# Retention attention and a top-1 expert layer on one core: x's rows a block later, the last three blocks routed as one group, weight pieces in other blocks

## The chip, the cores and the metric

The kernel runs on one core of a Trainium2 chip. The metric is device time in microseconds (us) for one execution, of which the median of several runs is given. The core has five engines that each work through their own instructions in order: TensorE (PE, with its weight loads PEld), VectorE (DVE), ScalarE (ACT), GpSimd (POOL) and SyncE (SP, which here only issues DMA transfers). They wait for each other by semaphores. An engine's order is fixed when the kernel is built, so an instruction that waits holds up all that stand behind it on its engine.

## The reference, cut to what matters

```python
# q, k, v: (4, 8, 768, 64); gamma = 1 - 2**(-5 - head)
for t in range(S):
    state = gamma * state + k[t] v[t]^T        # per batch and head, 64 x 64
    y[t] = scale * q[t] @ state
x = y as (3072 tokens, 512)                     # 8 heads x 64
idx = argmax(x/|x| @ (emb/|emb|).T / tau)       # 1 of 8 experts for each token
gate = softmax(...)[idx]
out = gate * (relu(x @ w1[idx]) @ w2[idx])      # w1 512x1024, w2 1024x512
```

Every token goes through one expert only. So tokens have to be counted and sorted by expert, and the rows of x gathered in that order, before an expert's matmuls can start.

## The kernel before, in words

*Attention (lines 860 to 935).* The 3072 tokens are 24 blocks of 128 (NB = 24, six to a batch). The loop over n runs blocks 0 to 22, and block 23 follows behind it by hand, with the first matmuls of the experts already woven in. A block on PE is: `scores` (L349), transposes of the next q and k (L322, L337), `state` (L371), `logits` of the block before (L444), `inter` (L390) and `intra` (L399). DVE multiplies the scores by the causal mask in two halves (`masks`, pm, L356), which `intra` reads. ACT copies the result to xT (`take`). DVE turns xT into rows (`rows`, x, L414), which SP stores to DRAM as xd, two blocks at a time; ACT squares them and DVE sums them (`squares`, `sums`, L431) for the norms. POOL scales q and v (L309, L315). In the kernel before, `rows(n - 1)` and `sums(n - 2)` are called at the end of block n.

*Routing.* For groups of blocks, `to_rows` (PE, L540) and `choose` (DVE, L556 to L570, eight instructions) find the expert of each token, `count` (PE, L578 to L582) counts, `ranks` and `place` (DVE, L589 to L476) give each token its place in its expert's list, `marks_of` prepares the last factor (L489 on POOL, L492 on DVE), and `fill` (PE, L512) with `add_to_table` (DVE, L522 to L525) adds the group to the table of token numbers. Tables are filled at n = 12, n = 18 and n = 21 (18 blocks: the early rows) and once more behind block 23. `pad()` (L603) then makes up the first expert's count to 288 early rows. The blocks behind the early ones are routed in three groups: A = 18 to 20, BB = 21 and 22, CC = 23.

*The hand-over.* `xge` holds the first 288 rows of expert 0, gathered from xd as soon as the table of the early rows stands (L531). `early_rows` transposes them (L669) and splits each number into a high and a low part (xh, xl), since every product of the experts is made of three matmuls: whi with xh, whi with xl, wlo with xh. `products()` is the list of expert 0's single matmuls on the early rows: 96 of the first layer (L219) and 24 for each column block dt of the second (L954). `run(m)` issues m of them, and the tuple R says how many stand at each of the places between the routing steps. `weave` issues several lists of routing instructions in turn.

*Late rows and expert 1.* Behind the last table the 128 late rows of expert 0 are gathered (L1019), transposed (L1040), and run through the first layer (L1055); ACT and DVE make hh and hl of them (L1070), and `late_rows` (L1190, 24 matmuls) is their second layer. `gather(1)` (L236) fetches the rows of expert 1 from xd, they are stored to xs and read back as xg (L246, L252), DVE transposes them (xt, L1114), ACT and DVE split them (xh, xl, L1116, L1118), and expert 1's first layer follows. The gates are gathered as gt (L1090) and multiply the result (L1195). Expert e+2 is gathered while e runs.

*Weights.* A weight piece is 128 x 1024 numbers, eight to an expert. `load_piece` asks SP for the next (512 KB), `split_piece(engine, parts)` lets ACT cast it to whi (L194) and the named engine subtract the two for wlo (L195). Up to the seam POOL does the subtracting in two halves of 128 x 512.

*What sets the order.* In the attention loop and in the seam the instructions of each engine stand as the code issues them, and lists of jobs (`mids`, `lates`, `ends`) put routing steps at fixed places of fixed blocks. In the part behind it a scheduler moves instructions of one engine past each other where their data allow it, so that the diff alone does not tell what stands first.

## Time and profile before

| | |
|---|---|
| three runs | 445.16, 446.98 and 448.91 us; median 446.98 |
| profiled execution | 448.59 us, of which the profile spans 446.8 |
| PE busy | 411.7 us (92% of the span), 3535 matmuls |
| DVE, ACT, POOL busy | 257.3, 177.8, 215.6 us (58%, 40%, 48%) |
| mean clock granted to PE | 0.976 of full speed |
| DMA | 88.16 MB, mean 197 GB/s |

The profile is of one execution. Times in it are us from the span's start. An engine's row in a timeline gives its start, its length, the line of the kernel, the operation with the tiles that it writes and reads, how many alike are merged (x4), and in brackets for how long the engine had been idle and which instruction or transfer ended this. Matmuls overlap, so the length of one is more than its distance to the next. Attention runs to about 127 us, the seam from there to about 156, and the experts from there to the end.

### The profile page before, as it was taken

The numbers are of one execution on the slowest core, as the hardware profiler recorded it, in microseconds if no ns is written. First come the engines' busy times: TensorE is split into PE (matmuls) and PEld (weight loads), VectorE is DVE, ScalarE is ACT, GpSimd is POOL, SyncE is SP. The second block draws the span as 40 slices with busy tenths as digits, with TensorE's granted clock in tenths as the row PEclk, the third lists the DMA queues.
The fourth block names the chain that finished last, engine by engine and source line by source line (L and its number), as shares of the span: only waits on it lengthen the run. The fifth ranks groups of instructions, "written<-read, shape, count | busy, mean of one in ns | idle before, by whom it ended". The sixth has DMA issues, their size and how long they took to land.

```text
span 446.8 us, 9424 instructions
## 1 busy us (share of the span) xinstructions
PE 411.7 (92%) x3535; PEld 366.4 (82%) x3535; DVE 257.3 (58%) x546; ACT 177.8 (40%) x324; POOL 215.6 (48%) x206
## 2 busy tenths in 40 slices
PE   7999999999897997889999989999999989999960
PEld 4778787777677995689999989999999869889840
DVE  4356786787867773645653584385476285755110
ACT  2455646455454152523342253254244244524000
POOL 2574557585549033582674367347445542350010
PEclk9999999999998999899999999999999999999995
DMA  7999999999862398479579959779979999410010
GB/s 169 239 243 231 218 235 221 234 259 229 228 182 46 109 294 228 120 207 298 171 243 170 296 204 223 183 278 228 259 255 235 284 298 238 173 71 19 27 45 2
DMA packets 119747, 88.16 MB, mean 197 GB/s; under 512 B 58512, under 2 KB 101432, under 8 KB 119692
## 3 DMA queue, kind: packets, MB, share of 16 engines
q1 hardware_dynamic: 114516, 74.52, 64.4%
q0 software_dynamic: 5088, 12.93, 9.4%
q8 instruction: 30, 0.49, 0.5%
q14 instruction: 25, 0.20, 0.1%
q10 hardware_dynamic: 88, 0.02, 0.0%
HBM read 65.08 MB, written 18.59 MB: 187 GB/s over the span
## 4 chain that ended last, share of the span: by engine, by line
PE 58%; DMA 18%; DVE 8%; SPq 6%; issue 4%; ACT 3%; POOL 0%; POOLq 0%; DVEq 0%; ACTq 0%
PE psc L219 10%; PE py L219 10%; DMA raw<-in_moe_w_dram 8%; PE psc L349 5%; PE py L1179 5%; PE py L399 5%; PE py L1135 4%; PE psc L1135 4%; PE psc L1179 2%; SPq L1154 2%; PE pq L322 2%; PE pst L371 2%; PE py L390 2%; PE pk L337 2%; DMA hl<-in_k_dram 2%
## 5 line engine op out<-in xcount | busy, mean ns | idle before, releaser
L195 DVE TENSOR_TENSOR wlo<-raw,whi 128x1024 fp32r<-128x1024 f32 x56 | 69.4, 1241 | 48.9 <-ACT whi L194 43.3
L194 ACT CAST whi<-raw 128x1024 fp32r<-128x1024 f32 (+1 forms) x72 | 67.2, 951 | 45.0 <-DMA raw<-in_moe_w_dram 41.5
L1166 POOL DMA_INDIRECT out_dram<-og,sidx x28 | 31.6, 1129 | 93.7 <-DVE og L1203 29.3
L219 PE MATMUL py<-xh,whi 128*128 128x384 f32 (+5 forms) x128 | 44.3, 346 | 8.3 <-ACT xh L1116 5.7
L219 PE MATMUL psc<-xh,whi 128*128 128x384 f32 (+5 forms) x128 | 43.9, 343 | 2.3 <-DVE hl L223 2.3
L219 PE MATMUL py<-xl,whi 128*128 128x384 f32 (+5 forms) x128 | 44.3, 346 | 1.1 <-DVE xl L1118 0.9
L1160 POOL TENSOR_SCALAR og<-og,gt 128x512 f32<-128x512 f32 (+4 forms) x19 | 33.7, 1773 | 22.6 <-DMA og<-yt 12.9
L219 PE MATMUL psc<-xl,whi 128*128 128x384 f32 (+5 forms) x128 | 43.9, 343 | 0.0
L219 PE MATMUL psc<-xh,wlo 128*128 128x384 f32 (+5 forms) x128 | 43.7, 342 | 0.0
L219 PE MATMUL py<-xh,wlo 128*128 128x384 f32 (+5 forms) x128 | 43.5, 340 | 0.0
L1090 POOL DMA_INDIRECT gt<-gd,tidx x28 | 32.8, 1171 | 15.5 <-issue 7.9
L236 POOL DMA_INDIRECT xr<-xd,tidx x25 | 28.0, 1122 | 22.7 <-DMA xs<-xr 9.5
L356 DVE TENSOR_TENSOR pm<-psc,cst 128x512 f32<-128x512 f32 x48 | 30.8, 682 | 13.7 <-PE psc L349 13.6
L219 PEld LDWEIGHTS py<-xh,whi 128*128 128x128 f32 x128 | 24.5, 192 | 10.4 <-ACT xh L1116 7.2
L222 ACT ACTIVATE hh<-psc 128x384 fp32r<-128x384 f32 (+5 forms) x32 | 15.7, 491 | 43.1 <-PE psc L219 43.1
L223 DVE SCALAR_TENSOR_TENSOR hl<-psc,hh 128x384 fp32r<-128x384 f32 (+5 forms) x32 | 17.7, 553 | 24.6 <-ACT hh L222 24.5
L222 ACT ACTIVATE hh<-py 128x384 fp32r<-128x384 f32 (+5 forms) x32 | 15.7, 491 | 40.6 <-PE py L219 38.9
L399 PE MATMUL py<-pm,vs 128*64 128x128 f32 x384 | 29.1, 286 | 1.8 <-DVE pm L356 1.7
L349 PE MATMUL psc<-qT,kT 64*128 64x128 f32 x384 | 28.3, 286 | 0.4 <-ACT qT L326 0.4
L1116 ACT CAST xh<-xt 128x384 fp32r<-128x384 f32 (+4 forms) x28 | 13.7, 523 | 37.3 <-DVE xt L1114 37.3
L223 DVE SCALAR_TENSOR_TENSOR hl<-py,hh 128x384 fp32r<-128x384 f32 (+5 forms) x32 | 17.6, 551 | 18.1 <-ACT hh L222 17.9
L399 PEld LDWEIGHTS py<-pm,vs 128*64 128x64 f32 x384 | 22.2, 140 | 6.9 <-DVE pm L356 3.2
(296 smaller groups left out, 994.6 us busy)
## 6 DMA issues: line engine op xcount, KB each, us to landing
raw<-in_moe_w_dram SPq DMA_DIRECT2D x46, 512.0 KB, 6.3
raw<-in_moe_w_dram SPq DMA_DIRECT2D x28, 256.0 KB, 5.4
xd<-x SPq DMA_DIRECT2D x48, 128.0 KB, 3.8
hl<-in_k_dram SPq DMA_DIRECT2D x23, 256.0 KB, 5.1
hh<-in_q_dram SPq DMA_DIRECT2D x11, 512.0 KB, 7.9
xs<-xr SPq DMA_DIRECT2D x7, 768.0 KB
xg<-xs SPq DMA_DIRECT2D x16, 208.0 KB, 5.9
xg<-in_v_dram SPq DMA_DIRECT2D x12, 256.0 KB, 4.9
```

Of the source, the lines that this page charges most:

```text
L194: nc.scalar.copy(out=hv, in_=rv)
L195: eng.tensor_tensor(out=lv, in0=rv, in1=hv.bitcast(F32), op=ALU.subtract)
L219: nc.tensor.matmul(acc[:, :w], a[:, f], x[:, kt, cols], start=(n == 0), stop=(n == 3 * KT - 1))
L222: nc.scalar.activation(out=hh[:, ft, cols], in_=acc[:, :w], func=AF.Relu)
L223: nc.vector.scalar_tensor_tensor(out=hl[:, ft, cols], in0=acc[:, :w], scalar=0.0, in1=hh[:, ft, cols].bitcast(F32), op0=ALU.max, op1=ALU.s ...
L349: nc.tensor.matmul(psc[par][:, j, :], kT[r, j, :], qT[r, j, :], start=True, stop=True)
L399: nc.tensor.matmul(py[j % 2][half(h), j // 2, :], vs[:, h, :], pt[a][:, j, :], start=(c == 0 and j < 2), stop=True, skip_group_check=True)
L1090: nc.gpsimd.indirect_dma_start(out=gt, out_offset=None, in_=gd[:, :], in_offset=bass.IndirectOffsetOnAxis(ap=idx, axis=0), bounds_check=NT ...
L1135: nc.tensor.matmul(acc[:, :CAPS[e]], a[:, f], x[:, kt, :CAPS[e]], start=(n == 0), stop=(n == 3 * FT - 1), skip_group_check=True)
L1160: nc.gpsimd.tensor_scalar(out=og[:n, j], in0=og[:n, j], scalar1=gts[e][:n, j:j + 1], scalar2=None, op0=ALU.mult)
L1166: nc.gpsimd.indirect_dma_start(out=out[:, :], out_offset=bass.IndirectOffsetOnAxis(ap=sidx[:n, j, e:e + 1], axis=0), in_=og[:n, j, :], in_ ...
L1179: nc.tensor.matmul(acc[:s, :], x[:, kt, g], a[:, f], start=(n == 0), stop=(n == 3 * FT - 1))
```

## The change

- In the loop, `rows(n - 2)`, `squares(n - 3)` and `sums(n - 4)` now stand right behind block n's masks; before, the rows and sums stood at a block's end and one and two blocks earlier.
- Weight pieces are loaded at n = 8, 14, 19, 20, 22 (before: 5, 9, 13, 16, 21, 22) and split at the ends of n = 11, 17, 21, 22 (before: 8, 12, 16, 19). Three pieces are loaded and three split on POOL around block 23, and the eighth piece is split on DVE behind the gather of the late rows.
- `pad` takes its place in PSUM as an argument and moves from the end of n = 21 to n = 22, behind group A's `to_rows`; group A is chosen at the end of n = 22, and counted, ranked and placed within block 23.
- Blocks 21 to 23 are one group BB; the group CC of block 23 alone is gone.
- R becomes (12, 8): 12 single products behind BB's choice, 16 more woven one at a time into BB's chain (`slowly`), then 8, then the table. The remaining ones come behind it.
- The second layer's dt = 1 leaves `products()` and is issued with dt = 2 and 3, behind `gather(1)`.

```diff
--- before.py
+++ after.py
@@ -44,7 +44,7 @@
 assert LATE == P and EARLY % P == Q and CAPS[0] % P == Q
 NBE = 3 * NC_
 NKIN = 6
-R = (2, 3, 5, 14, 56)
+R = (12, 8)
 W0 = 8
 STRIDE = 3200
 NOV = (NT - OV + P - 1) // P
@@ -596,9 +596,8 @@
 
         quarters = cp.tile([P, P], F32, name="quarters")
 
-        def pad():
-
-            cn = work[:, 2 * P:]
+        def pad(cn):
+
             ex = cn[:, 2 * NE:2 * NE + 1].broadcast_to([P, len(range(0, QE, NQ))])
             nc.tensor.matmul(cn[:, :NE], ones, cum[:, NBE, :], start=True, stop=True)
             nc.vector.tensor_scalar(out=cn[:, 2 * NE:2 * NE + 1], in0=cn[:, :1], scalar1=-1.0, scalar2=float(EARLY),
@@ -858,7 +857,7 @@
         scale_v(0)
         scale_q(0, 1)
         scale_v(1)
-        A, BB, CC = slice(NBE, NBE + 3), slice(NBE + 3, NB - 1), slice(NB - 1, NB)
+        A, BB = slice(NBE, NBE + 3), slice(NBE + 3, NB)
         for r, n, m in ((slice(0, 6), 7, 8), (slice(6, 12), 13, 13), (slice(12, 15), 16, 16), (slice(15, NBE), 19, 19)):
             choosing(r, n, m)
         for r, n, m, tag in ((slice(0, 6), 9, 10, "a"), (slice(6, 12), 14, 15, "b"), (slice(12, 15), 17, 17, "a"),
@@ -879,7 +878,7 @@
                 load_k(n + 4)
             if n % 2 == 0 and n // 2 + 3 < NB // 2:
                 load_q(n // 2 + 3)
-            if n in (5, 9, 13, 16, 21, 22):
+            if n in (8, 14, 19, 20, 22):
                 load_piece()
             psc = scores(n)
             if n > 0:
@@ -888,7 +887,11 @@
             if n == 0:
                 next(emb_steps)
             if n > 1:
-                squares(n - 2)
+                rows(n - 2)
+            if n > 2:
+                squares(n - 3)
+            if n > 3:
+                sums(n - 4)
             if 3 < n < NB - 3:
                 scale_q((n + 1) // 2 + 1, (n + 1) % 2)
             if n > 0:
@@ -902,7 +905,9 @@
                     transpose_q(n // 2 + 1, 0 if n == 3 else n % 2)
                 transpose_k(n + 1)
             run_jobs(mids, n)
-            last = n == NB - 2
+            if n == NB - 2:
+                psA = to_rows(range(A.start, A.stop), psT.tile([P, 512], F32, name="pq"))
+                pad(psA[:, 3 * P:])
             if n % NC_ < NC_ - 1:
                 state(n)
             if n > 0:
@@ -913,8 +918,6 @@
             py = inter(n)
             if n == 1 or n == 3:
                 transpose_q(n // 2 + 1, 1)
-            if last:
-                psA = to_rows(range(A.start, A.stop), psT.tile([P, 512], F32, name="pq"))
             intra(n, py, pt)
             if n == 0:
 
@@ -928,13 +931,9 @@
                 nc.gpsimd.tensor_tensor(out=tri, in0=C("causal"), in1=ident, op=ALU.subtract)
                 nc.gpsimd.tensor_scalar(out=quarters, in0=slots, scalar1=C("inq"), scalar2=None, op0=ALU.is_equal)
             run_jobs(ends, n)
-            if n > 0:
-                rows(n - 1)
-            if n > 1:
-                sums(n - 2)
-            if n == NBE + 3:
-                pad()
-            if n in (8, 12, 16, 19):
+            if n == NB - 2:
+                weave(choose(A, psA))
+            if n in (11, 17, 21, 22):
                 split_piece(nc.gpsimd, 2)
 
 
@@ -961,8 +960,7 @@
             for ft in range(FT):
                 yield from first_layer(0, ft, bank(), xh0, xl0, hh0, made["hl"], first)
             made["yt"] = hp.tile([P, NXC, KT, Q], F32, name="xg")
-            for dt in range(KT // 2):
-                yield from second_layer(dt)
+            yield from second_layer(0)
 
         todo = products()
 
@@ -970,44 +968,44 @@
             for _ in range(m):
                 next(todo, None)
 
+        def slowly(m):
+
+            for _ in range(m):
+                run(1)
+                yield
+
         n = NB - 1
-        for _ in range(2):
+        for _ in range(3):
             load_piece()
         psc = scores(n)
         take(n - 1, py)
         pt = masks(psc)
-        weave(choose(A, psA))
-        squares(n - 2)
+        rows(n - 2)
+        squares(n - 3)
         logits(n - 1)
+        prA = count(A, psA, 192)
         py = inter(n)
         intra(n, py, pt)
         take(n, py)
-        prA = count(A, psA, 192)
+        weave(chain(ranks(A, prA), place(A, "a", prA)))
+        early_rows(0, "pk")
+        early_rows(1, "psc0")
+        logits(n)
         psB = to_rows(range(BB.start, BB.stop), psT.tile([P, 512], F32, name="pst"))
-        for kt, tag in enumerate(("pk", "psc0", "psc1", "pk")):
-            early_rows(kt, tag)
+        early_rows(2, "psc1")
+        early_rows(3, "pk")
+        weave(marks_of(range(A.start, A.stop)))
         weave(choose(BB, psB))
-        for _ in range(2):
+        for _ in range(3):
             split_piece(nc.gpsimd, 2)
         rows(n - 1)
+        squares(n - 2)
+        sums(n - 4)
         run(R[0])
         prB = count(BB, psB, 192)
+        weave(chain(ranks(BB, prB), place(BB, "b", prB), marks_of(range(BB.start, BB.stop), prB)), slowly(16))
+        rows(n)
         run(R[1])
-        logits(n)
-        rows(n)
-        run(R[2])
-        psC = to_rows([n])
-        weave(choose(CC, psC))
-        weave(chain(ranks(A, prA), place(A, "a", prA), marks_of(range(A.start, A.stop))))
-        run(R[3])
-        prC = count(CC, None, 192)
-        squares(n - 1)
-        weave(chain(ranks(BB, prB), place(BB, "b", prB), marks_of(range(BB.start, BB.stop), prB)))
-        weave(chain(ranks(CC, prC), place(CC, "c", prC), marks_of(range(n, NB), prC)))
-        squares(n)
-        for _ in range(2):
-            split_piece(nc.gpsimd, 2)
-        run(R[4])
         tb = add_to_table(B - 1, fill(B - 1, "pq"))
 
         xr = hp.tile([P, DM], F32, name="xr")
@@ -1019,6 +1017,10 @@
         nc.gpsimd.indirect_dma_start(
             out=xr, out_offset=None, in_=xd[:, :], in_offset=bass.IndirectOffsetOnAxis(ap=lidx, axis=0),
             bounds_check=NT - 1, oob_is_err=False)
+        split_piece(nc.vector, 2)
+        sums(n - 3)
+        for m in (n - 1, n):
+            squares(m)
 
         todo2 = counting()
         for i in range(14):
@@ -1032,6 +1034,7 @@
             nc.vector.tensor_copy(out=ldst[a:z], in_=sidx[a:z, j, :1])
         for m in range(n - 2, NB):
             sums(m)
+            run(6)
         run(3 * KT * FT * 2)
         hl0, yt0 = made["hl"], made["yt"]
         r = slice(EARLY, CAPS[0])
@@ -1221,12 +1224,13 @@
                 next(gate_steps)
                 og = mp.tile([P, NG, DM], F32, name="og", bufs=2)
                 xT_tiles(1)
-                for dt in range(KT // 2, KT):
+                for dt in range(1, KT):
                     for _ in second_layer(dt):
                         pass
-                    if dt == KT // 2:
+                    if dt > 1:
+                        xT_pieces(1, (2 * dt - 4, 2 * dt - 3))
+                    else:
                         split_piece()
-                    xT_pieces(1, (2 * dt - 4, 2 * dt - 3))
                 split_piece()
                 acc0, og0 = late_rows(), og
                 gather(2)
```

On DVE, within attention blocks 14 and 15, the order before is this (pm are the masks, x the rows, ssq the sums, parts the logits, ohbb a placing step).

```order
L414 STREAM_TRANSPOSE x<-xT 128x4x4x32
L431 TENSOR_REDUCE ssq_73<-sq 128x4
L356 TENSOR_TENSOR pm_1419<-psc_1406,cst_61 128x512
L356 TENSOR_TENSOR pm_1421<-psc_1407,cst_61 128x512
L446 STREAM_TRANSPOSE parts<-aux 128x128
L457 TENSOR_TENSOR aux<-aux,cst_61 128x96
L460 TENSOR_REDUCE aux<-aux 128x6
L462 SCALAR_TENSOR_TENSOR aux<-wmx,aux 128x6
```

And now, at the same place:

```order
L356 TENSOR_TENSOR pm_1399<-psc_1386,cst_61 128x512
L356 TENSOR_TENSOR pm_1401<-psc_1387,cst_61 128x512
L414 STREAM_TRANSPOSE x<-xT 128x4x4x32
L431 TENSOR_REDUCE ssq_73<-sq 128x4
L446 STREAM_TRANSPOSE parts<-aux 128x128
L457 TENSOR_TENSOR aux<-aux,cst_61 128x96
L460 TENSOR_REDUCE aux<-aux 128x6
L462 SCALAR_TENSOR_TENSOR aux<-wmx,aux 128x6
```

The transpose of x and the sum have moved from ahead of the two masks to behind them.

On POOL, from the gathers of the early rows to the gather of expert 1's rows, the order before is this (vs is block 23's scaled v, xl the low part of the early rows, wlo a half of a split, at the marks).

```order
L531 DMA xr<-xd,g_2068 32x512
L315 TENSOR_TENSOR vs<-xl,cst_60 128x512
L673 TENSOR_TENSOR xl<-qs,xh 128x288 x4
L195 TENSOR_TENSOR wlo<-raw,whi 128x4x4x32 x4
L489 TENSOR_SCALAR at<-marks,rla,cst_61 128x32 x3
L195 TENSOR_TENSOR wlo<-raw,whi 128x4x4x32 x2
L195 TENSOR_TENSOR wlo<-raw_2164,whi 128x4x4x32 x2
L1019 DMA xr<-xd,lidx 128x512
L236 DMA xr<-xd,tidx 128x512 x3
```

And now:

```order
L531 DMA xr<-xd,g_2051 32x512
L195 TENSOR_TENSOR wlo<-raw,whi 128x512 x2
L315 TENSOR_TENSOR vs<-xl,cst_60 128x512
L195 TENSOR_TENSOR wlo<-raw_1853,whi 128x512 x2
L672 TENSOR_TENSOR xl<-qs,xh 128x288 x4
L489 TENSOR_SCALAR at<-marks,rla,cst_61 128x32 x3
L195 TENSOR_TENSOR wlo<-raw,whi 128x4x4x32 x6
L1017 DMA xr<-xd,lidx 128x512
L236 DMA xr<-xd,tidx 128x512 x3
```

Two halves of a split now stand between the gathers and block 23's v, two more behind it, and six behind the marks.

On DVE, around the late rows of expert 0 and the first of expert 1's rows, the order before is this (hl of pst and pk is the late rows' low part, xt the transposed rows of expert 1, which read xg, the rows that a transfer brings).

```order
L195 TENSOR_TENSOR wlo<-raw,whi 128x1024
L803 TENSOR_REDUCE aux<-aux 1x8
L805 CAST cnti<-aux 1x8
L807 CAST cnti<-aux 1x8
L1070 SCALAR_TENSOR_TENSOR hl<-pst,hh 128x4x128
L1070 SCALAR_TENSOR_TENSOR hl<-pk,hh 128x4x128
L1114 STREAM_TRANSPOSE xt<-xg 128x416 x2
L1118 TENSOR_TENSOR xl<-xt,xh 128x416 x2
```

And now (lines have moved by three):

```order
L195 TENSOR_TENSOR wlo<-raw,whi 128x1024
L956 STREAM_TRANSPOSE xg<-psc_2753 128x9x32
L802 TENSOR_REDUCE aux<-aux 1x8
L1117 STREAM_TRANSPOSE xt<-xg 128x416 x2
L804 CAST cnti<-aux 1x8
L806 CAST cnti<-aux 1x8
L1073 SCALAR_TENSOR_TENSOR hl<-pst,hh 128x4x128
L1073 SCALAR_TENSOR_TENSOR hl<-pk,hh 128x4x128
L1121 TENSOR_TENSOR xl<-xt,xh 128x416 x2
```

The first two transposes of expert 1's rows have moved from behind the late rows' hl to ahead of it. On PE the late rows' matmuls stand ahead of expert 1's first layer in both.

## Rows read from the trace of the kernel before

**Rows 1.** Who waited for whom: PE, 60 to 195 us.
```profile
engine line waited for: us in total, times, longest us
PE py L219 <- ACT xh L1116: 2.9, 1, 2.9
PE py L219 <- DVE og L1195: 2.6, 1, 2.6
PE psc L219 <- DVE hl L223: 2.3, 1, 2.3
PE py L399 <- DVE pm L356: 1.7, 4, 1.0
PE pk L337 <- DMA hl<-in_k_dram: 1.2, 1, 1.2
PE aux L603 <- DVE g L644: 1.1, 1, 1.1
```

**Rows 2.** Busy time by windows: blocks 14, 15, 18, 21, and the seam.
```profile
core 0: us, PE busy (x) PEld busy (x) DVE busy (x) ACT busy (x) POOL busy (x), PEclk, DMA share, GB/s
75.80:82.12 6.32, 5.16 (x90) 4.03 (x88) 3.35 (x8) 3.01 (x8) 3.18 (x4) 1.00 1.00 238
82.12:86.83 4.71, 4.71 (x85) 3.81 (x81) 4.28 (x14) 2.29 (x7) 2.00 (x2) 1.00 0.93 227
96.01:102.10 6.09, 4.90 (x91) 3.81 (x88) 4.53 (x14) 2.66 (x8) 4.60 (x7) 1.00 1.06 246
111.90:117.98 6.08, 5.56 (x107) 4.30 (x105) 4.53 (x14) 2.72 (x8) 3.48 (x6) 1.00 0.82 163
117.98:156.59 38.61, 34.63 (x370) 30.29 (x369) 28.79 (x116) 14.75 (x36) 19.81 (x21) 0.96 0.46 139
```

**Rows 3.** Timeline of POOL, from block 23's v to expert 1's gather.
```profile
123.13 1.05 POOL L315 TENSOR_TENSOR vs<-xl,cst 128x512 f32<-128x512 f32 x1
129.70 3.18 POOL L673 TENSOR_TENSOR xl<-qs,xh 128x288 fp32r<-128x288 f32 x4 [5.52 <-ACT xh L672]
...
137.86 1.40 POOL L489 TENSOR_SCALAR at<-marks,rla,cst 128x32 f16<-128x32 f16 x3
...
149.23 1.11 POOL L1019 DMA_INDIRECT xr<-xd,lidx  x1 [5.04 <-issue]
156.59 1.00 POOL L236 DMA_INDIRECT xr<-xd,tidx  x1 [6.25 <-PE py L540]
```

**Rows 4.** POOL by line: splits, and scaling of results (ns min/median/max, first and last start).
```profile
L195 POOL TENSOR_TENSOR wlo<-raw,whi x16: 1263/1284/1317, 51.5 to 142.9; 128x512 fp32r<-128x512 f32 x16
...
L1160 POOL TENSOR_SCALAR og<-og,gt x19: 1562/1581/2587, 194.9 to 368.2; 128x512 f32<-128x512 f32 x14, 32x512 f32<-32x512 f32 x2, 24x512 f32<-24x512 f32 x1, 16x512 f32<-16x512 f32 x1
```

**Rows 5.** ACT by line and shape: half casts (busy us, mean ns, idle before).
```profile
L194 ACT CAST whi<-raw 128x512 fp32r<-128x512 f32 x16 | 9.0, 627 | 0.0
```

**Rows 6.** Timeline of DVE: BB's chain, late rows' hl, expert 1's rows.
```profile
137.19 0.17 DVE L589 TENSOR_TENSOR pst<-pst,oh 128x16 f32<-128x16 f32 x1
...
139.38 0.41 DVE L492 SCALAR_TENSOR_TENSOR at<-marks,rlb,pst 128x32 f16<-128x32 f16 x2
...
170.11 0.69 DVE L1070 SCALAR_TENSOR_TENSOR hl<-pst,hh 128x512 fp32r<-128x512 f32 x1
...
178.07 1.10 DVE L1114 STREAM_TRANSPOSE xt<-xg 128x416 f32<-128x416 f32 x2 [6.66 <-DMA xg<-xs]
```

**Rows 7.** Timeline of PE: block 23, late rows, start of expert 1.
```profile
125.64 1.58 PE L399 MATMUL py<-pm,vs 128*64 128x128 f32 x16
...
170.13 0.50 PE L1190 MATMUL py<-whi,hh 128*128 128x512 f32 x1
...
176.06 0.39 PE L1190 MATMUL py<-wlo,hh 128*128 128x512 f32 x1
179.31 0.46 PE L219 MATMUL py<-xh,whi 128*128 128x416 f32 x1 [2.86 <-ACT xh L1116]
...
183.34 0.35 PE L219 MATMUL py<-xh,whi 128*128 128x416 f32 x1
```

**Rows 8.** The chain that ended last: second layer of the early rows, expert 1.
```profile
149.48 6.40 PE psc L954 x48
...
191.21 3.87 PE py L219 x19
```

## The prediction, made before the changed kernel was run

> **What bounds the kernel now.** I read the page first, then the list of who waited for whom, then windows of single blocks, and last the timelines of PE, POOL and DVE around the hand-over from attention to the experts. TensorE (PE) is the bound: in a steady block it is busy without a gap [rows 2], so the change can be worth only what PE waits, or what PE works longer than it must. Behind 60 us the list of its waits is short [rows 1]: between 60 and 195 us some 12 us, each with one name. The reader is to see that these waits lie at places that the diff touches, and that none is longer than 3 us.
>
> The windows tell block from block [rows 2]. A steady attention block (n=15, from 82.12) takes 4.71 us, and PE is busy for all of it. Block 14, before it, takes 6.32 us with PE busy for 5.16: it waited 1.2 us for a k load [rows 1], with the DMA engines at a share of 1.00. Block 18 (from 96.01) takes 6.09 us with 4.90 busy: it waited for DVE's masks. Block 21 (from 111.90, up to the table's matmuls) takes 6.08 with 5.56 busy. The stretch from there to the gather of expert 1's rows takes 38.61 us with PE busy for 34.63.
>
> From that gather on, a chain of transfers is the path. The gathers start at 156.59 us [rows 3], their rows are written to DRAM and read back, and DVE can transpose the first of expert 1's rows at 178.07 us [rows 6], 21.5 us after the first gather. PE has filler for most of this time (the late rows, 24 products, the last of them at 176.06) and then waits 2.86 us [rows 7].
>
> **The change, part by part.** The terms are set against the profiled execution's own time, 448.59 us, which is 1.61 above the median of the three runs, 446.98; what comes off the one is then taken off the other.
>
> *Loads later in the loop.* Before, three weight pieces have been asked for by block 13; now one, and the second in block 14. A piece is 512 KB; at the 238 GB/s of block 14's window [rows 2] that is 2.2 us of transfers less ahead of each k load behind it. The wait of block 14 can so go wholly or not at all (1.16 or 0, 6.32 less 5.16); I take 1.16, as 2.2 is more than the delay.
>
> *Rows and sums behind the masks.* DVE's order shows the two masks now first in a block, and the transpose of x and the sum behind them. The wait for masks goes: 1.19 us in block 18 (6.09 less 4.90) and 0.52 in block 21 (6.08 less 5.56). The x rows come a block later, but nobody in the loop waits for them: the stores that they feed are read only by gathers much later.
>
> *Splits later in the loop.* POOL now splits a piece at the end of block 17. In the window of block 18 POOL was busy for 4.60 of 6.09 us [rows 2]. Two halves of 1.28 us [rows 4] come into it, 7.2 us in all, where the block without its wait lasts 4.9. POOL's scaling of q and v stands behind the halves, and PE's transposes of q wait for that. It costs nothing if POOL's slack in the blocks around covers it, and 2.3 us (7.2 less 4.9) if none does; the 1.5 us of slack in the window lie in part behind the halves, and I take 1.0.
>
> The loop so gives 1.16 + 1.19 + 0.52 - 1.0 = 1.9 us (bounds -0.6 and 2.9).
>
> *The seam.* Of PE's 34.63 busy us the second layer's column block dt=1 goes behind the gather: 24 products, of which 48 took 6.40 us [rows 8], so 3.2 us. The small matmuls of the group of one block go too, some 0.3 by my estimate. 31.1 us of work are left. All 3.98 us of waiting (38.61 less 34.63) end as they are today: the pad's matmul (1.1 us behind the table [rows 1]) is now asked for a block later, when DVE has long delivered; and the 2.3 us for DVE's hl [rows 1] stood behind the routing chains of two groups, of which one is gone. Two new waits come.
>
> First, POOL: between the three gathers of the early rows and the scaling of v for block 23 there now stand two halves of a split. Before, the scaling began at 123.13 and took 1.05 us [rows 3]; with 2.5 us ahead of it, it ends at 126.7. PE began the product of block 23 that reads it at 125.64 [rows 7], and without the pad's wait, with choosing in between, it comes there some 0.3 us sooner: a wait of 1.4 us. The ends are 0 (if PE is later there than I think) and 2.5 (all of the halves).
>
> Second, the three-block group: the chain of its two-block forerunner ran on DVE from 137.19 to 139.8 [rows 6], 2.6 us. Now PE has 16 + 8 products (3.2 us) to run beside it, and then needs its marks for the table. In the middle of the chain stands an hl that waits for ACT, and ACT has six half casts of 0.63 us [rows 5] ahead of it, 3.8 us in all. If that hl is on time, the chain ends about when the products do, and PE waits some 0.2 us; if it holds the chain for 3.8 less the 1.2 us or so in which ACT can begin before, PE waits 2.8. I take the upper end, since the casts are in program order ahead of it. POOL's part is no later: 126.7 and two halves more, xl (3.2), marks (1.4) [rows 3] and six halves (7.7) end at 141.5. The gather of the late rows behind them began at 149.23 [rows 3] with its reader at 155.88 [rows 8], so 6.6 us are enough; the reader now comes at 152.6, and the gather may start as late as 146.
>
> The seam then takes 31.1 + 1.4 + 2.8 = 35.3 us against 38.61, so 3.3 less, and so much sooner does expert 1's gather begin.
>
> *Behind the gather.* The second layer's dt=1 now fills 3.2 us of the wait for transfers, so PE should stand still for less. But DVE's order shows what the diff does not: the transposes of expert 1's rows (L1117) now stand ahead of the late rows' hl (L1073). Before, hl ran at 170.11 [rows 6], long before the rows landed; now it stands behind an instruction that waits for the landing. PE's 24 late products wait for hl, and expert 1's products stand behind them on PE. From the start of the transposes to expert 1's fourth group of products it took 191.21 - 178.07 = 13.1 us [rows 6, 8]. Now these follow each other: two transposes 1.10, two small casts 0.2, one hl 0.69 [rows 6], together 2.0; the 24 late products, which ran from 170.13 to 176.06 [rows 7] at some 0.24 each, 5.7 (all at half the clock 11.4; I take 7.3, by the next paragraph); and 36 products of expert 1 at 0.19, 6.8. The sum is 16.1 us (14.5 to 20.2), 3.0 more. The gates' gather, for which PE waited 2.6 us at this place [rows 1], is then done in time.
>
> On the clock: after the wait of 2.86 us PE's nine products of 416 columns took 4.03 us, from 179.31 to 183.34 [rows 7], 0.45 each; after the wait of 2.6 us ahead of 191.21, 19 products took 3.87, 0.20 each [rows 8]. So I price half speed for three to four us after such a wait, 1.6 us lost.
>
> *Further on* the experts' phase is the same in both, with weights loaded as PE frees them; it shifts by what stands above.
>
> Sum: 1.9 + 3.3 - 3.0 = 2.2 us. 448.59 - 2.2 = 446.4 on the profiled execution's scale, 446.98 - 2.2 = 444.8 on that of the median.
>
> **The rivals.**
>
> *A: the transfers are quicker.* The weights that share the queue with the row chain are asked for sooner, and less may lie beside it. Whatever shortens the 21.5 us from gather to rows [rows 3, 6] starts the late rows sooner by as much, up to the 6 us for which PE otherwise stands ahead of them (its filler ends at about 170, the hl comes at about 176). Half of it, 3 us, gives 441.8. For it speaks that this wait is purely one of transfers; against it, that the queues carry the same bytes in the same order.
>
> *B: the loop gives nothing.* If the k load is late all the same (the second piece falls into the very block that stalled) and POOL's scaling takes all that the masks gave, the 1.9 us go: 446.7, no change. For it speaks POOL's 4.60 of 6.09 us; against it the 2.2 us of loads taken out.
>
> *C, the other side: POOL's halves become slow beside a busy DVE.* Ten halves now stand ahead of the late rows' gather behind the early ones, where eight stood before. A half has taken 1.263 to 1.317 us, but scaling a tile of 128x512 took 1.56 to 2.59 us later in the kernel [rows 4]. With h the length of a half, POOL is free at 141.5 + 10 (h - 1.28), and the gather may start at 146, so it decides from h = 1.7 on. At the worst of the rows, 2.59, POOL is free at 154.6, 8.6 us late, and the whole chain with it; at 2.4 it is 6.7: 444.8 + 6.7 = 451.5. Against it: the 16 halves of the trace, in the loop and in the seam, all lie within 0.06 us. The Trainium skill (GPSIMD Engine Reference, section 8. Key points) says that this engine shares its SBUF interfaces with VectorE, with contention when DVE runs instructions with two SBUF inputs; by that rule C would be the likely case. The trace's halves, which ran beside a busy DVE, do not show it.
>
> **How the numbers follow.** I give the forecast 0.45, A 0.27, B 0.17, C 0.11. A measurement of this kernel tells about 1% from no change, 4.5 us: 442.5 and 451.5. Faster: 0.2 of the forecast's cases (its terms off by 2.3 us together) and 0.8 of A's, 0.09 + 0.22 = 0.31. Slower: half of C's and 0.08 of the forecast's and B's (the late products wholly at half clock with both new waits at their upper ends), 0.055 + 0.05 = 0.10. The rest, 0.59, is no change. The range goes from 439 (A with nearly all of its 6 us) to 450 (C from h = 2.2 is left out, and so are the worst of the bounds): about one case in ten is left out on either side.
>
> **What would show it.** In the changed profile: no wait of PE for pm in block 18 and none for a k load in block 14; PE's q transposes of block 19 late by about 1 us; the pad's matmul without a wait; a wait for vs ahead of block 23's last products (1.4); a wait ahead of the last table's matmuls (2.8); the late products behind expert 1's transposes, with PE idle for about 6 us ahead of them. I am wrong if the late hl runs before the rows land, if POOL's halves take more than 1.7 us, or if the landing comes much less than 21 us behind the gather.

## The result, and the profile after

The changed kernel took 444.3 us (median of 21 runs, 441.06 to 448.56) where the kernel before took 449.15 (21 runs, 445.16 to 455.53): a ratio of 0.9899, 95% interval 0.9871 to 0.9928, so 4.5 us less. The forecast was 444.8 us, 2.2 less than before. Two more groups of runs give less: 1.0013 (0.9973 to 1.0053) and 1.0006 (0.9958 to 1.0054), with medians 3.4 and 1.0 us below those of the kernel before. A ratio counts only the runs within 1.5% of the fastest of each kernel (in the first of these two groups 11 of 12 against 14 of 35), so it can show no change where the medians of all runs lie 3.4 us apart. The kernel before, timed against itself over 12 runs, came out at 1.000 (0.993 to 1.0069), while its median was 452.04 against 449.0. A single group of runs therefore tells 1% at best, and the main evidence below is the profiles, of which there are now fourteen.

The profiled execution of the changed kernel took 442.79 us (span 440.9). First the list of who waited for whom, PE from 55 to 195 us; it answers to [rows 1].

```profile
engine line waited for: us in total, times, longest us
PE py L1193 <- DVE hl L1073: 6.6, 1, 6.6
PE py L399 <- POOL vs L315: 2.1, 1, 2.1
PE pq L512 <- DVE at L492: 1.6, 1, 1.6
PE aux L444 <- ACT xT L406: 0.6, 1, 0.6
PE aux L512 <- DVE parts L446: 0.5, 2, 0.3
...
PE pq L322 <- POOL qs L309: 0.4, 1, 0.4
```

The reader is to see that every name has changed. The waits for pm, for k, for g, for the first products' hl and, at expert 1, for xh and og are gone; in their place stand the three that the prediction named (the late hl with 6.6 us, v with 2.1, the marks ahead of the last table with 1.6) and small ones that it did not name. Then the windows of blocks 14, 18 and 19, and of the seam from the table of the early rows to expert 1's gather, as in [rows 2].

```profile
core 0: us, PE busy (x) PEld busy (x) DVE busy (x) ACT busy (x) POOL busy (x), PEclk, DMA share, GB/s
74.50:79.47 4.97, 4.97 (x90) 4.05 (x88) 3.36 (x9) 2.91 (x8) 1.29 (x2) 1.00 0.95 232
...
93.36:98.65 5.29, 4.90 (x91) 3.90 (x89) 4.53 (x14) 3.53 (x10) 4.36 (x6) 1.00 1.02 239
98.65:104.03 5.38, 4.96 (x98) 3.97 (x88) 4.56 (x15) 1.95 (x5) 4.67 (x6) 1.00 0.96 206
...
114.05:150.78 36.73, 31.56 (x358) 26.94 (x344) 27.73 (x100) 17.32 (x42) 22.22 (x22) 0.95 0.66 184
```

Block 14 lost its 1.35 us and block 18 lost 0.8, of which block 19 gave 0.5 back (4.90 us before). The seam holds 31.56 us of PE's work (31.1 forecast) and lasts 36.7 (35.3 forecast). POOL in the seam, which answers to [rows 3]:

```profile
116.67 1.26 POOL L531 DMA_INDIRECT xr<-xd,g  x1 [3.46 <-DVE pm L356]
...
120.51 2.50 POOL L195 TENSOR_TENSOR wlo<-raw,whi 128x512 fp32r<-128x512 f32 x2
122.97 1.04 POOL L315 TENSOR_TENSOR vs<-xl,cst 128x512 f32<-128x512 f32 x1
...
131.73 7.48 POOL L195 TENSOR_TENSOR wlo<-raw,whi 128x512 fp32r<-128x512 f32 x6
142.46 1.11 POOL L1017 DMA_INDIRECT xr<-xd,lidx  x1 [3.25 <-DVE hl L223]
150.78 1.00 POOL L236 DMA_INDIRECT xr<-xd,tidx  x1 [7.22 <-PE psc L540]
```

Two halves stand ahead of v as the order said, and each of the ten takes some 1.25 us, no more than before [rows 4]. At the late rows, PE's timeline, as in [rows 7]:

```profile
167.25 0.50 PE L1193 MATMUL py<-whi,hh 128*128 128x512 f32 x1 [0.25 <-ACT hh L1072]
174.32 0.80 PE L1193 MATMUL py<-whi,hl 128*128 128x512 f32 x1 [6.57 <-DVE hl L1073]
...
181.16 0.35 PE L219 MATMUL py<-xh,whi 128*128 128x416 f32 x1
...
187.97 0.35 PE L219 MATMUL py<-xh,whi 128*128 128x416 f32 x1
```

and DVE's, as in [rows 6]:

```profile
172.46 1.10 DVE L1117 STREAM_TRANSPOSE xt<-xg 128x416 f32<-128x416 f32 x2 [5.42 <-DMA xg<-xs]
...
173.60 0.67 DVE L1073 SCALAR_TENSOR_TENSOR hl<-pst,hh 128x512 fp32r<-128x512 f32 x1
```

DVE stands at the transposes until expert 1's rows land, and the late hl runs behind them, 1.14 us after they began. PE waits 6.57 us, the late products take 6.84 from then on, and expert 1's fourth group starts at 187.97, 15.5 us after the transposes (13.1 before, 16.1 forecast).

To see where an execution gains and loses I cut each profile at the same four instructions: the scores of blocks 1 and 22, expert 1's gather, the first transpose of its rows, and its second layer; the last piece ends with PE's last product. In us:

| profile of | block 1 to 22 | to gather | to transpose | to 2nd layer | to the last product |
|---|---|---|---|---|---|
| before | 104.5 | 37.5 | 21.5 | 24.6 | 228.5 |
| before_again | 103.3 | 37.4 | 21.6 | 23.9 | 228.1 |
| after | 100.5 | 36.6 | 21.7 | 26.9 | 226.3 |
| after_again | 101.0 | 39.3 | 22.6 | 26.9 | 223.0 |
| after_third | 104.2 | 38.7 | 22.6 | 28.1 | 228.5 |
| forecast, after less before | -2.9 | -2.3 | 0 | +3.0 | 0 |

(The forecast's 1.05 us for the pad lies ahead of block 22's scores, so it is counted in the first piece here.) The last piece of after_third holds stalls of another kind, told at the end.

### The profile page after: what moved, and what is told of

It is laid out like the page before. It is cut to its first block, busy times and chain, and to the rows that moved or that the text cites. A ratio compares the mean times of both kernels' runs of the same rounds, so it can differ in the third digit from the quotient of the medians.

```text
span 440.9 us, 9397 instructions
## 1 busy us (share of the span) xinstructions
PE 407.3 (92%) x3526; PEld 365.2 (83%) x3526; DVE 256.4 (58%) x530; ACT 177.4 (40%) x324; POOL 210.1 (48%) x204
## 5 line engine op out<-in xcount | busy, mean ns | idle before, releaser
L195 DVE TENSOR_TENSOR wlo<-raw,whi 128x1024 fp32r<-128x1024 f32 (+1 forms) x58 | 71.4, 1234 | 38.8 <-ACT whi L194 35.0
L1093 POOL DMA_INDIRECT gt<-gd,tidx x28 | 31.2, 1115 | 16.3 <-issue 8.2
L222 ACT ACTIVATE hh<-py 128x384 fp32r<-128x384 f32 (+5 forms) x32 | 15.5, 489 | 48.5 <-PE py L219 46.9
L223 DVE SCALAR_TENSOR_TENSOR hl<-py,hh 128x384 fp32r<-128x384 f32 (+5 forms) x32 | 17.6, 553 | 24.9 <-ACT hh L222 24.6
L309 POOL TENSOR_TENSOR qs<-hh,cst 128x512 f32<-128x512 f32 x23 | 23.9, 1042 | 13.3 <-DMA hh<-in_q_dram 11.3
L399 PE MATMUL py<-pm,vs 128*64 128x128 f32 x384 | 27.1, 279 | 2.7 <-POOL vs L315 2.1
L349 PE MATMUL psc<-qT,kT 64*128 64x128 f32 x384 | 28.1, 285 | 0.4 <-ACT qT L326 0.4
L1119 ACT CAST xh<-xt 128x384 fp32r<-128x384 f32 (+4 forms) x28 | 13.7, 523 | 35.6 <-DVE xt L1117 35.6
L399 PEld LDWEIGHTS py<-pm,vs 128*64 128x64 f32 x384 | 20.8, 136 | 7.4 <-POOL vs L315 2.4
```

Of the source, the lines that this page charges most:

```text
L195: eng.tensor_tensor(out=lv, in0=rv, in1=hv.bitcast(F32), op=ALU.subtract)
L222: nc.scalar.activation(out=hh[:, ft, cols], in_=acc[:, :w], func=AF.Relu)
L223: nc.vector.scalar_tensor_tensor(out=hl[:, ft, cols], in0=acc[:, :w], scalar=0.0, in1=hh[:, ft, cols].bitcast(F32), op0=ALU.max, op1=ALU.s ...
L349: nc.tensor.matmul(psc[par][:, j, :], kT[r, j, :], qT[r, j, :], start=True, stop=True)
L399: nc.tensor.matmul(py[j % 2][half(h), j // 2, :], vs[:, h, :], pt[a][:, j, :], start=(c == 0 and j < 2), stop=True, skip_group_check=True)
L1093: nc.gpsimd.indirect_dma_start(out=gt, out_offset=None, in_=gd[:, :], in_offset=bass.IndirectOffsetOnAxis(ap=idx, axis=0), bounds_check=NT ...
```

## The experiments

**The changed kernel again, twice.** No edit.

> The changed kernel as it is, for comparison on the same chip. Both theories: ratio to the kernel before 0.990 (0.987 to 0.993). What it also decides: in the first pair of profiles the changed kernel was 1.0 us ahead by the second block already, and 2.0 us ahead at expert 3's first layer, where the kernel before waited twice. If these belong to the change, they return here; if they are the luck of one execution, the lead at block 1 is under 0.3 us, or PE waits at expert 3 here too.

> The changed kernel as it is once more, for comparison within this group and as a third profile. Median about 444.8 us. If the waits named so far belong to it: PE waits 2.1 to 2.4 us for block 23's v and 6.5 to 7.5 us for the late rows' hl; block 14 waits for no k; whether the clock falls behind the wait for v is open (it did in one of two profiles).

Measured: medians 445.37 and 450.21 us. The lead of 1.0 us at block 1 was the luck of the first profile of the kernel before (before_again reached block 1 in 13.48 us, the changed kernel in 13.63). The waits for v (2.41 and 0.87 us) and for the late hl (7.47 and 7.52) return, the first shrinking where PE itself comes late. What the prediction did not have in the seam is the clock. In after_again, windows of 4 us from the wait for v on:

```profile
122.00:126.00 4.00, 1.59 (x28) 1.35 (x22) 2.41 (x11) 0.00 (x0) 4.00 (x5) 0.71 0.96 331
126.00:130.00 4.00, 3.56 (x31) 1.94 (x28) 0.36 (x2) 2.15 (x6) 2.62 (x4) 0.50 0.64 203
130.00:134.00 4.00, 4.00 (x16) 3.21 (x17) 2.70 (x10) 2.99 (x8) 2.54 (x5) 0.50 0.60 185
134.00:138.00 4.00, 4.00 (x24) 3.85 (x23) 1.64 (x8) 2.56 (x6) 4.00 (x5) 0.58 0.00 0
```

PEclk (third number from the end) is 0.50, the lower of the two levels, for 13.7 us in all (the four windows added up), and the first products of the experts, which stood there, take 0.24 us each instead of 0.13. From block 22 to expert 1's gather it took 39.3 us instead of 36.6, although no wait ahead of the table was left. After_third has a spell as long. In the first profile the clock stayed up behind the wait for v, and fell for 3.4 us only at the wait ahead of the last table (windows of after):

```profile
134.00:138.00 4.00, 2.43 (x34) 1.99 (x33) 3.66 (x17) 1.12 (x3) 4.00 (x5) 0.81 0.01 2
138.00:142.00 4.00, 4.00 (x25) 4.00 (x25) 3.28 (x10) 1.01 (x3) 1.21 (x1) 0.77 0.59 131
```

Both profiles of the kernel before have 3.4 us of half clock in the seam too. It is not shown that the wait for v brings the long spells. In after_third the whole window from 126.00 on is at 0.50, and PE's wait for v began only at 126.39 (127.26 less 0.87):

```profile
122.00:126.00 4.00, 3.25 (x44) 2.19 (x44) 2.59 (x11) 2.32 (x5) 3.67 (x4) 1.00 1.01 289
126.00:130.00 4.00, 3.13 (x31) 2.08 (x23) 2.67 (x12) 0.74 (x2) 3.64 (x4) 0.50 0.86 313
```

```profile
127.26 1.98 PE L399 MATMUL py<-pm,vs 128*64 128x128 f32 x16 [0.87 <-POOL vs L315]
```

**The late hl first.** The late rows' transposes, hh and hl are issued behind the early rows' dt = 2:

```diff
-        for f in range(2):
-            pt = psT.tile(...)
...
+        def late_split():
+            for f in range(2):
+                pt = psT.tile(...)
...
+                    if dt == 2:
+                        late_split()
```

> The late rows' transposes, hh and hl are issued behind the second column block of the early rows, ahead of expert 1's transposes on DVE; nothing else. Theory (the 6.6 us wait of PE stands there only because hl is queued behind the transposes that wait for expert 1's rows): PE's 24 late products run during the transfer, the wait for hl falls from 6.6 to under 0.5 us, PE then waits about 4 us for expert 1's rows, and from the first of these transposes to expert 1's fourth group of products it takes 13.1 us instead of 15.5, with a wait for the gates there again: 2.2 us less than the changed kernel, ratio to the kernel before 0.985. Rival (the transfer chain alone sets the time, and the gates' gather ends at the same moment anyway): the fourth group starts within 0.5 us of where it does, ratio 0.990.

Measured: median 445.02, ratio 0.9908 (0.9856 to 0.9959). DVE and PE in its profile:

```profile
169.09 0.69 DVE L1075 SCALAR_TENSOR_TENSOR hl<-pst,hh 128x512 fp32r<-128x512 f32 x1
...
177.81 1.10 DVE L1120 STREAM_TRANSPOSE xt<-xg 128x416 f32<-128x416 f32 x2 [7.30 <-DMA xg<-xs]
```

```profile
179.05 0.46 PE L219 MATMUL py<-xh,whi 128*128 128x416 f32 x1 [1.32 <-ACT xh L1122]
...
190.22 0.45 PE L219 MATMUL py<-xh,whi 128*128 128x416 f32 x1 [0.66 <-DVE og L1201]
```

hl runs 8.7 us ahead of the transposes, the wait for it is gone, and from the transposes to expert 1's second layer it takes 23.9 us instead of 26.9. At its place the theory is shown: the order on DVE alone cost 3.0 us there. In the median against after_again (445.37) it is not seen, and the ratio is the one that the rival named: the profile lost 1.3 us in the loop against that of after_again and 2.9 in the last piece, where expert 6 waited 2.2 us for its rows (not at all in after_again).

**The third piece's split ahead of the gathers, and both edits.**

```diff
+            if n == 21:
+                split_piece(nc.gpsimd, 2)
             run_jobs(lates, n)
...
-            if n in (11, 17, 21, 22):
+            if n in (11, 17, 22):
```

> The third piece's split moves on POOL from behind the early rows' gathers to ahead of them, where POOL was idle for 3.5 us; nothing else. Theory (two halves in POOL's order between the gathers and block 23's v cost PE 2.1 us): the wait of PE for v falls from 2.1 to 0.2 us, the early rows' low parts come 2 us sooner, and expert 1's gather begins some 1.9 us sooner after the table of the early rows (34.8 instead of 36.7 us); ratio to the kernel before 0.986. Rival (the wait only moves to the chain of the last group, where PE waited 1.6 us already): the wait ahead of the last table grows from 1.6 to over 3 us and the stretch keeps more than 36.2 us; ratio 0.990.

> late_first and early_split together. If the two waits are independent: 4.1 us less than the changed kernel, ratio to the kernel before 0.981. If expert 1's transfers and the gates bound both, no better than the better of the two alone, 0.985.

Measured: 445.11 (0.9966, 0.9924 to 1.0008) and 445.29 (0.9956, 0.9917 to 0.9995). PE in early_split:

```profile
121.97 1.09 PE L399 MATMUL py<-pm,vs 128*64 128x128 f32 x16 [0.20 <-POOL vs L315]
124.04 0.33 PE L668 MATMUL pk<-ident,xr 128*128 128x128 f32 x1 [0.98 <-DMA xr<-xd,g]
126.47 0.51 PE L668 MATMUL pk<-ident,xr 128*128 128x128 f32 x2 [2.10 <-DMA xr<-xd,g]
```

The wait for v fell to 0.20 us as expected, and 3.1 us of waiting for the early rows took its place: the wait has moved, though not to where the rival had put it (0.19 us ahead of the table). The wait for v had covered the landing of the gathers. From block 22 to expert 1's gather it took 38.5 us, where the theory had expected less than the 36.6 of after. With both edits the gain of late_first was seen again (24.1 us in the fourth piece), and nothing in the time.

**One edit of the loop at a time.** Rows, squares and sums as in the diff above, on the kernel before; the loads and splits in the new blocks, on the kernel before; the loads and splits in the old blocks, on the changed one; and the kernel before once more.

> The kernel before with only x's rows, squares and sums moved behind the masks a block later; weights, pad and groups as before. Theory (the wait for masks belongs to this edit, the k wait to the pieces): no wait for pm in blocks 18 and 21 (1.7 us less), the k wait of block 14 or one like it stays (0.5 to 1.5 us), the hand-over as before (38.6 us from the table to expert 1's gather, within 0.7); ratio 0.996. Rival (the loop is set by transfers, so what the masks gave is lost at the next k or v): block 22 starts less than 0.7 us sooner.

> The kernel before with only the weight pieces loaded and split in the new blocks (five in the loop and three behind it; splits at 11, 17, 21, 22 and two in the seam). Theory: no k wait in block 14 (1.2 us less), the masks' waits stay, a wait for block 23's v of about 2 us comes (two halves ahead of it on POOL) and the early rows' gathers take 6 us and more to land instead of 4.6, since weights now lie beside them; net 0 to 1 us slower, ratio 1.000 to 1.003. Rival (the pieces' new places are what made the changed kernel faster): over 2 us faster, 0.994.

> The changed kernel with the pieces' loads and splits in the blocks of the kernel before (six loads in the loop and two behind it; splits at 8, 12, 16, 19), all else as changed. Theory (in the changed kernel the splits cost at the seam what the loads save in the loop): the wait for block 23's v goes (2.1 to 2.4 us), so the clock does not fall before the first products, gathers land in under 5 us, and from the table to expert 1's gather it takes under 36 us; a k wait of about 1.2 us comes back in the loop. Ratio to the kernel before 0.985, 1 to 3 us below the changed kernel. Rival (loads in the loop cost more than that): 0.992 or above.

> The kernel before as it is, timed against itself. Ratio 1.00; how far it lies from 1.00 tells what the spread of this kernel does to a ratio. In the profile: if the waits of the first profile belong to the kernel, block 14 waits about 1.2 us for a k load again, block 18 1.2 us for the masks, and expert 3 and expert 6 wait about 1.4 and 2.1 us for their rows; if they are the luck of one execution, the block of the k wait and the experts' waits differ.

Measured: rows_later 450.01 us (1.013, 1.008 to 1.0179), new_pieces 445.74 (0.9941, 0.9884 to 0.9999), old_pieces 447.13 (0.9996, 0.9949 to 1.0043), beside 449.0 for the kernel before. None of the three theories held. The rows alone gained nothing: the median is 1.0 us above that of the kernel before, and from block 1 to 22 the profile took 106.7 us, where the two of the kernel before took 104.5 and 103.3. The pieces' new places alone came out 3.3 us lower by median, which is hardly more than the 3.0 us by which the kernel before differed from itself in this group, and took 103.2 us from block 1 to 22. The nine profiles with both edits took 100.5 to 104.2 there. In old_pieces the wait for v was gone, as expected, but PE waited 2.0 us for the early rows at the same place, the clock stood at half for 6.8 us from 129.3 on, and from block 22 to expert 1's gather it took 37.5 us: its rival. In the other two, as well, the numbers came out as the rivals had them. The waits of PE in rows_later, from its timeline:

```profile
70.08 0.37 PE L512 MATMUL aux<-ohba,at 128*32 128x32 f16 x24 [0.93 <-DVE parts L446]
...
93.63 0.63 PE L337 MATMUL pk<-ident,hl 128*128 128x128 f32 x4 [1.56 <-DMA hl<-in_k_dram]
...
109.23 0.63 PE L337 MATMUL pk<-ident,hl 128*128 128x128 f32 x4 [0.94 <-DMA hl<-in_k_dram]
113.53 0.17 PE L578 MATMUL aux<-cum,ones 128*128 128x24 bf16 x1 [1.08 <-DVE parts L446]
```

No wait for pm is left (before_again had 1.6 us of them, at the same blocks 18 and 21 as the first profile). But PE now waits for `parts`, which frees the PSUM bank of the counts and tables and has come to stand behind x and the sum on DVE: 2.3 us in this profile. And k waits are not tied to block 14: in the four profiles with the old places they came to 1.2, 0, 2.7 and 1.5 us, at different blocks, in the ten with the new places to 0 in three and 0.2 to 1.9 in the others (all from 55 us on).

Last, the gathers of the early rows. The table (g) and POOL's first gather stood 0.44 us apart before (118.84 and 119.28), 0.45 in rows_later and in new_pieces, but 1.5 to 2.9 in the changed kernel's three profiles and in seam. SP before, and after:

```profile
107.21 2.85 SPq L420 DMA_DIRECT2D xd<-x  x4
...
114.81 3.08 SPq L420 DMA_DIRECT2D xd<-x  x4
```

```profile
107.52 2.33 SPq L165 DMA_DIRECT2D raw<-in_moe_w_dram  x4
109.95 3.23 SPq L420 DMA_DIRECT2D xd<-x  x4
...
113.72 2.02 SPq L165 DMA_DIRECT2D raw<-in_moe_w_dram  x4
115.83 2.02 SPq L420 DMA_DIRECT2D xd<-x  x4
```

The stores of blocks 16 and 17, the last that the early rows need, were issued by 110.06 before; now they stand behind four loads of a piece and are issued by 113.18, 3.5 us ahead of the first gather (3.3 to 5.5 in the other profiles with both edits). That the gather stood behind the landing of these stores is argued from the order: the profiles put POOL's wait there down to other names (DVE's pm, loads of weights and of v). From issue to landing the three gathers then take 5.4 to 6.2 us where they took 3.6 to 4.7; in the other profiles with both edits 6.3 to 7.8 where it is recorded, in rows_later 6.0 to 7.7, in old_pieces 6.5 to 7.6, in new_pieces 3.9 to 5.0. So the slow landing comes with the rows, not with the weights that I had blamed in the expectation; that the next pair's stores lie beside the gathers fits this, but it was not tried by itself.

**Both edits of the loop without the hand-over, and a mended hand-over.** loop_only is rows_later and new_pieces together. In seam the last four loads (one of block 22, three ahead of block 23) go behind block 21's stores, the third piece is split behind v, the fourth on DVE:

```diff
-            if n in (8, 14, 19, 20, 22):
+            if n in (8, 14, 19, 20):
...
-            if n in (11, 17, 21, 22):
+            if n in (11, 17, 22):
...
-        for _ in range(3):
-            load_piece()
...
         squares(n - 3)
+        for _ in range(4):
+            load_piece()
...
         intra(n, py, pt)
+        split_piece(nc.vector, 2)
```

> The kernel before with both edits of the loop (rows a block later, pieces in other blocks) and its old hand-over (pad in block 21, three groups, 80 products ahead of the table, second layer's dt=1 ahead of the gather). Theory (the gain of the changed kernel is made in the loop, and the new hand-over gives back what it saves): within 1.5 us of the changed kernel's median, 443.5 to 446.5. Rival (the hand-over brings a good part): 2 us or more above the changed kernel's median, 447 or more.

> The changed kernel with three edits at the hand-over: the third piece is split on POOL behind block 23's v instead of ahead of it, the fourth on DVE, and the last four pieces are loaded behind the stores of block 21 instead of beside the early rows' gathers. Theory (the wait for v, the slow landing of the gathers and the fall of the clock behind them are what the hand-over pays): PE's wait for v under 0.3 us, gathers land in under 5.5 us (5.4 to 7.8 in the changed kernel and its variants), no half clock before the first products, and from block 22's start to expert 1's gather 34.5 to 36 us (36.6 to 39.7); median 2 us below the changed kernel's. Rival (something else comes due there, a cast or a weight that lands late): over 37 us, median within 1 us.

> The same three edits, and the late rows' hl ahead of expert 1's transposes. Theory: the two gains add, since they lie on one path: 3.0 us less between expert 1's transposes and its second layer (23.9 instead of 26.9 us) on top of the 2 us, median 4 to 5 us below the changed kernel's, about 440. Rival (waits of the later experts for their rows, 0 to 6 us in the profiles so far, take up what comes sooner): median less than 2 us below the changed kernel's.

Measured: 451.11, 450.89 (1.0053, 1.0001 to 1.0105) and 452.74 us (0.999, 0.9904 to 1.0076), beside 450.21 for the changed kernel and 451.19 for the one before. None of the three is shown to be faster than the changed kernel. In seam the wait for v is gone, but this is what PE shows:

```profile
125.87 1.59 PE L399 MATMUL py<-pm,vs 128*64 128x128 f32 x16 [0.56 <-DVE pm L356]
...
131.62 0.32 PE L540 MATMUL pst<-parts,quarters 128*32 128x24 f32 x8 [2.72 <-DVE parts L446]
```

The split on DVE (2.14 us) stands ahead of group A's chain and that ahead of `parts`, for which PE now waits 2.72 us; the gathers began at 120.68, 2.9 us behind their table, and the half clock came again (6.8 us). When the gathers landed is not recorded there. From block 22 to the gather it took 38.9 us: the rival. With the late hl first as well (seam_late) the fourth piece takes 26.0 us instead of seam's 28.8. Loop_only, with the old hand-over, took 38.5 for the second piece and 23.9 from the transposes to the second layer, against 38.7 and 28.1 of after_third. Its median lies within 1 us of the changed kernel's, but over six runs that spread from 442 to 457 us, so that the pieces of one profile support the theory and the time hardly does.

## Why the prediction was right, and where it was not

*Time.* 444.8 was forecast and 444.3 measured, but the difference of 2.2 us came out as 4.5 in the first comparison, and between 1 and 3.4 in the medians of the repeats. That the forecast came so close is in good part luck. The first four pieces of the table hold all that it priced; they add up to 188.1 and 186.1 us in the two profiles before and to 185.7, 189.8 and 193.6 in the three after, so that together they show no sure gain where 2.2 us were forecast. In the mean of the first two on either side these pieces are 0.6 us longer after than before, and what after and after_again have ahead lies in the last piece, which the forecast put at nothing (see *Further on*).

*Masks.* Right where it was looked for: no wait for pm in blocks 18 and 21 in any profile with the edit (1.6 to 1.7 us without it). One step failed: "nobody in the loop waits for them". I followed the x rows to their readers, but not the instruction that had been pushed behind them: `parts` came later by the length of x and the sum, and PE's counts and tables wait for its bank, 0.5 us in after and 2.3 in rows_later.

*Pieces.* I took the k wait of block 14 as a property of the kernel. It is a matter of the single execution: 1.35 us on average over four profiles with the old places (0 to 2.7), 0.66 over ten with the new (0 to 1.9). The sign was right and the size of 1.16 about twice too large by these rows; the medians give the pieces more (3.3 us, new_pieces against the kernel before), which is no more than the noise of that group and which the profiles do not explain.

*POOL in block 18.* 1.0 us forecast, 0.4 to 0.7 measured as waits for q in block 19.

*Seam.* Forecast 3.3 us less, measured 1.9 less once; in the two repeats it took, from the table's matmuls on, 0.6 us more than before and the same. (By the pieces above, which begin behind the pad's wait, 2.3 less was forecast, and 0.8 less, 1.9 and 1.3 more came.) PE's work and the two waits were there (v 2.1, marks 1.6 against 1.4 and 2.8). What failed is "read only by gathers much later": the early rows' gathers are the first readers of the stores, stand in the next block, and now start later and land later. And no loss of clock was priced in the seam, only at the late rows: two of three executions have 13.7 us of half clock there, the third 3.4, and the piece is 2.7 us longer in after_again than in after. What brings the longer spell stays open.

*Late rows.* Right in place, cause and size: 3.0 us forecast, 2.3 to 3.0 in after and after_again (3.5 to 4.2 in after_third, with a wait of 0.8 us for og besides), and 3.0 back in late_first.

*Further on.* "Shifts by what stands above" was wrong for the profiles: the last piece is 1.8 to 5.5 us shorter in after and after_again than in the two profiles before, in part as the experts waited less for their rows (expert 3 1.4 and 1.7 us before, never after; expert 6 0 to 2.6 us in both). In the mean of these two pairs it is 3.6 us shorter, and the whole table only 3.0. What makes it is not shown. It goes with the rows a block later: outside the last group, whose stalls are told below, it takes 223.0 to 226.3 us in the seven profiles with that edit (rows_later 224.9) and 228.1 to 229.3 in the three without (new_pieces 229.3). How an edit of the attention loop would reach the later experts was not followed.

*Rivals.* A did not come: the chain from gather to rows took 21.7 to 22.6 us. C did not either: POOL's halves took 1.25 to 1.32 us in all fourteen profiles. The Trainium skill (GPSIMD Engine Reference, section 8. Key points) would have them slower beside a DVE that reads two inputs; no profile here shows it, and in seam a half took 1.27 us with DVE's own two-input subtract beside it for 1.0 us. Of B, the part about POOL was small, and `parts`, which it did not name, took back 0.5 us of the masks' gain in after and all of it in rows_later.

## What to carry to other kernels

When a step is moved behind others on an engine, follow two things: its own readers, and every instruction that now stands in a new place behind it, down to who waits for the buffer that this one frees. Read the built order of instructions around each wait for a transfer: whatever stands behind the waiting instruction shares its wait, and the diff does not show it. Take a wait for a transfer in a loop that fills the DMA engines as a draw, not as a fixed price: it takes several profiles to tell what it costs. And before a forecast that came close is called right, add up the pieces of the profiles that it priced: here they do not show its gain.

## What was not expected of the hardware

At a wait of 2.1 us for v the clock stayed at its upper level (after); at one of 2.4 at the same place it fell to 0.50, for 13.7 us in after_again and 10.2 in late_first, though PE was busy again; in after_third it fell for 13.7 us while PE was still at work, 0.4 us ahead of its wait. After 2.6 us ahead of expert 1's fourth group it had not fallen at all [rows 8]. So the length of the wait alone does not decide.

On the last chip (after_third, loop_only, seam and seam_late) PE stood still in expert 2's first layer for 1.4 to 5.0 us with no releaser, "issue" in the list of waits, in four profiles of four and in none of the ten others. In after_third:

```profile
237.98 0.34 PE L219 MATMUL psc<-xh,whi 128*128 128x408 f32 x1 [0.38 <-issue]
239.38 0.35 PE L219 MATMUL psc<-xl,whi 128*128 128x408 f32 x1 [1.06 <-issue]
```

DVE had an instruction with such an idle time of 8.5 us there in the same profile. What the engines waited for is not shown; for comparisons it means that the last group of runs is to be read within itself only.
